# Moving score batches, queue order and the first output parts in a fused linear-attention and local-attention kernel

## The chip, the cores and the metric

The kernel runs on one core of one Trainium2 chip. The metric is the device time of one execution in microseconds (us); every kernel is run several times and the median of its runs is quoted. A profiled execution has a "span", which is about 1.7 us shorter than the time of the same run.

Names used below: PE is the matmul engine, PEld its weight loads, ACT is ScalarE, DVE is VectorE, SP is the engine whose queue issues most DMAs.

## The reference

Two attention blocks over the same input x (2048 x 1024) are mixed by a gate:

```python
g = sigmoid((x * gate_w).sum(-1, keepdims=True))
a = A(x, A_wqkv, A_wo)   # linear attention: phi(q) @ (phi(k)^T v) / den, 32 heads
b = B(x, B_wqkv, B_wo)   # each query sees 8 keys, 2 positions apart (dilated window), softmax
return g * a + (1 - g) * b
```

## The kernel before

It has three stages that matter here. Stage 1 (to 218 us) makes A's keys, values and normalized queries. The *window stage* (218 to 372 us) does B in eight chunks of four heads. Each chunk has two *quads* of 32 steps; a step is four 64x64 matmuls of 512 columns that run side by side and takes 0.216 us. A quad makes the keys `kt` and the queries `qz` of half of the sequence, in four PSUM banks. Between the steps stand, at fixed step numbers, five *score batches* per chunk (query times key, then exp on ACT, mask on DVE) and five *PV batches* (probabilities times V), each 14 steps after its scores. After the first half of an output's sum, one column of its bank is copied to `seen`, and the second half waits for that copy. The *output stage* (372 us to the end) sums, for each of 33 output parts, an A side (8 matmuls, `pqT` times `WoA`) and a B side (8 matmuls, `OBT` times `WoB`).

```python
# window stage: four outputs of a quad share steps; evictions follow the last step of a slot
def step(slot, kt):
    for j in range(2):
        for r in range(2):
            mm((slot + 2 * r) % 4, r, kt, j, slot < 2)       # 4 matmuls, 64x64
    if kt == KT - 1:
        for r in range(2):
            o = (slot + 2 * r) % 4
            if slot < 2:
                nc.vector.tensor_copy(out=seen[:], in_=banks[o][:, 0:1])   # one column
            else:
                outputs[o][2](banks[o])                                   # evict
# ... eviction of a query output: the same bank is read by ACT, then by DVE
nc.scalar.activation(out=qz[:, 0, par, :], in_=ps[:], func=ACT.Copy, scale=qsel[:, 0:1])
nc.vector.tensor_scalar(out=qz[:, 1, par, :], in0=ps[:], scalar1=qsel[:, 1:2], scalar2=None, op0=ALU.mult)
# ... positions of the five batches, in steps from the start of the chunk
p_ = 64 * c + (40, 52, 72, 84, 95)[m // 4]
events.append((p_, lambda g=g: scores(g)))
events.append((p_ + 14, lambda g=g: pv(g)))
# ... after the last batch of a chunk: results to DRAM, then one transposing load
nc.sync.dma_start_transpose(out=OBT[:, c, :], in_=obd[c][0:S, :])
# ... output stage
first = [out_part(*p_) for p_ in parts[:3]]
for k in range(2):                 # A sides of three parts, then their B sides
    for f in first:
        f(k)
```

PE, DVE and ACT run in program order in the window stage; the order of the SP queue is chosen by a scheduler.

Of the kernel before, what the change touches and what calls it, by code (L numbers as in the profile page):

```python
# [11 lines left out]
F32 = mybir.dt.float32  # L12
PE = mybir.EngineType.PE
DVE = mybir.EngineType.DVE
P = 128


# [21 lines left out]
def kernel(  # L39
# [11 lines left out]
    nc = tc.nc  # L51
# [40 lines left out]
    for i in range(4):  # L92
        if i == 2:
            nc.sync.dma_start_transpose(out=xT[:, :, P:2 * P], in_=rows(x, P, 2 * P))
        nc.sync.dma_start(out=WkA[0][:, 2 * i:2 * i + 2, :],
                          in_=A_wqkv[2 * i * P:(2 * i + 2) * P, D:D + 512].rearrange("(kt p) n -> p kt n", p=P))
    for t in range(2, NB):
        nc.sync.dma_start_transpose(out=xT[:, :, t * P:(t + 1) * P], in_=rows(x, t * P, (t + 1) * P))
# [44 lines left out]
    with tc.manual_schedule(engines={PE}):  # L143
# [191 lines left out]
            WqB = load_w("WqB", B_wqkv, 0, "wc")  # L335


        with ExitStack() as s2:
            ps_s = s2.enter_context(tc.tile_pool(name="ps_s", bufs=1, space=bass.MemoryType.PSUM))
            ps_o = s2.enter_context(tc.tile_pool(name="ps_o", bufs=1, space=bass.MemoryType.PSUM))  # L340
# [11 lines left out]
            s2.enter_context(tc.manual_schedule(engines={DVE, mybir.EngineType.Activation}))  # L352


            def quad_units(outputs):



                banks = {}

                def mm(o, r, kt, j, first):
                    if first and kt == 0 and j == 0:
                        banks[o] = ps_pj.tile([P, 512], F32, name="q4_ps", tag="pj")
                    lhsT, rhs, _ = outputs[o]
                    nc.tensor.matmul(banks[o][64 * j:64 * j + 64, :], lhsT=lhsT(r, kt, j), rhs=rhs(r, kt),  # L365
                                     start=first and kt == 0, stop=kt == KT - 1, skip_group_check=not first)
# [5 lines that stand above are left out]
                            mm(o, r, kt, j, slot < 2)  # L372
                    if kt == KT - 1:
                        for r in range(2):
                            o = (slot + 2 * r) % 4
                            if slot < 2:
                                nc.vector.tensor_copy(out=seen[:], in_=banks[o][:, 0:1])  # L377
                            else:
                                outputs[o][2](banks[o])
                for slot in range(4):  # L380
                    for kt in range(KT):
                        yield lambda slot=slot, kt=kt: step(slot, kt)
# [45 lines left out]
            def pv(g):  # L428
                c, m0, n = BATCHES[g]
                pt, base, ns = PT[g % 2], BLOCKS[m0][0], n // 2  # L430
                o2 = ps_o.tile([P, 2, 512], F32, name="o2", tag="o")[:, :, 0:ns * 132] \
                    .rearrange("p a (s i e) -> p a s i e", s=ns, i=4)
                for s_ in range(ns):
                    for i in range(4):
                        for dm in range(2):
                            for par in range(2):
                                m = m0 + 2 * s_ + dm
                                o = BLOCKS[m][0] - base
                                r = slice(64 * par, 64 * par + 64)
                                h = (dm + par) % 2  # L440
                                nc.tensor.matmul(o2[64 * h:64 * h + 64, par, s_, i, :], lhsT=pt[r, i, o:o + 64],  # L441
                                                 rhs=V[r, m, 4 * c + i, :], start=True, stop=True)
                part = m0 >= 8
                if m0 in (0, 8):
                    obs[part] = small.tile([P, 2, 5, P], BF16, name="Ob", tag="Ob")
                Ob = obs[part]
                s0 = m0 // 2 - 4 * part
                rd = small.tile([P, 2, 2, 4, 1], F32, name="rd", tag="rd")
                for a in range(2):
                    nc.vector.reciprocal(out=rd[:, a, 0:ns], in_=o2[:, a, :, :, Dh:Dh + 1])  # L450
                for a in range(2):
                    nc.vector.tensor_tensor(out=Ob[:, a, s0:s0 + ns, :].rearrange("p s (i e) -> p s i e", i=4),
                                            in0=o2[:, a, :, :, 0:Dh],
                                            in1=rd[:, a, 0:ns].broadcast_to([P, ns, 4, Dh]), op=ALU.mult)
                if m0 not in (4, 16):
                    return
                runs = ((0, 1), (1, 4), (2, 3)) if not part else ((8, 1), (9, 4), (10, 4), (17, 1))
                for par in range(2):
                    for m, k in runs:
                        h = (m + par) % 2  # L460
                        q0, w, _ = BLOCKS[m]
                        step = 2 * w if k > 1 else w
                        sl = m // 2 - 4 * part
                        nc.sync.dma_start(
                            out=obd[c][1024 * par + q0:1024 * par + q0 + k * step, :]
                            .rearrange("(s r) d -> r s d", r=step)[0:w],
                            in_=Ob[64 * h:64 * h + w, par, sl:sl + k, :])
                if part:
                    nc.sync.dma_start_transpose(out=OBT[:, c, :], in_=obd[c][0:S, :])

            events = []
            for g, (c, m, n) in enumerate(BATCHES):
                p_ = 64 * c + (40, 52, 72, 84, 95)[m // 4]
                events.append((p_, lambda g=g: scores(g)))
                events.append((p_ + 14, lambda g=g: pv(g)))

            def between(a, b):
                return [(p_ - a, f) for p_, f in events if a <= p_ < b]

            def quad(c, hh):  # L480
                outs = [kq_output(c, par, hh, which, kts[c], qzs[c, hh]) for par in range(2) for which in range(2)]
                return list(quad_units(outs))
            for c in range(KT):
                kts[c] = kpool.tile([P, 2, 1024], BF16, name="kt", tag="kt")
                for hh in range(2):
                    qzs[c, hh] = qpool.tile([P, 2, 2, 512], BF16, name="qz", tag="qz")
                    a = 64 * c + 32 * hh
                    interleave(quad(c, hh), between(a, a + 32))


            WoB = load_w("WoB", B_wo, 0, "wb")
            raw = wpool.tile([P, 4, D], BF16, name="raw", tag="wc")
            fw = wpool.tile([P, 2, D], F32, name="fw", tag="wc")
            lw = wpool.tile([P, 4, D], BF16, name="lw", tag="wa")
# [19 lines left out]

        with ExitStack() as s3:
            work3 = s3.enter_context(tc.tile_pool(name="work3", bufs=3))
            pqT.append(big.tile([P, KT, 1536], BF16, name="pqT1", tag="vV"))
            for r0 in (512, 1024):
                nc.sync.dma_start_transpose(out=pqT[2][:, :, r0 - 512:r0], in_=pqd[r0:r0 + 512, :])  # L519
# [7 lines left out]
                normalize(t, r, pn, fw[:, t % 2, :])  # L527
                nc.sync.dma_start_transpose(out=pqT[2][:, :, (t - 4) * P:(t - 3) * P], in_=pn)

            def out_part(tb, c0, n):  # L530

                st = {}

                def mm(side, c):
                    if side == 0 and c == 0:
                        st["ps"] = ps_pj.tile([P, 512], F32, name="d3_ps", tag="pj")
                    if side == 0:
                        lhsT, W = (pqT[tb // 2][:, c, (tb % 2) * P:(tb % 2 + 1) * P] if tb < 4 else
                                   pqT[2][:, c, (tb - 4) * P:(tb - 3) * P]), WoA
                    else:  # L540
                        lhsT, W = OBT[:, c, tb * P:(tb + 1) * P], WoB
                    nc.tensor.matmul(st["ps"][:, 0:n], lhsT=lhsT, rhs=W[c0 // 512][:, c, c0 % 512:c0 % 512 + n],  # L542
                                     start=(side == 0 and c == 0), stop=(side == 1 and c == KT - 1))
                    if side == 0 or c < KT - 1:
                        return
                    osb = work3.tile([P, 512], BF16, name="osb", tag="e")
                    nc.scalar.activation(out=osb[:, 0:n], in_=st["ps"][:, 0:n], func=ACT.Copy,  # L547
                                         scale=omg[:, tb:tb + 1])
                    nc.sync.dma_start(out=rows(out2, tb * P, (tb + 1) * P)[:, c0:c0 + n], in_=osb[:, 0:n])

                def side(k):
                    for c in range(KT):
# [2 lines left out]

            parts = [(tb, c0, n) for tb in range(NB)
                     for c0, n in ([(0, 512), (512, 512)] if tb < NB - 1 else [(0, 512), (512, 256), (768, 256)])]
            first = [out_part(*p_) for p_ in parts[:3]]
            for k in range(2):
                for f in first:  # L560
                    f(k)
            for i, p_ in enumerate(parts[3:]):
                if i % 2 == 1 and i < 8:
                    qa_late(12 + i // 2)
                f = out_part(*p_)
                f(0)
                f(1)


# [28 lines left out]
```

## Time and profile before

The median was 499.35 us when the prediction was made.

The page, for a span of 498.1 us, gives PE's busy time with its share, and in 40 equal slices PE's busy tenths and the granted clock of PE in tenths.

```profile
PE 473.5 (95%) x5748; PEld 249.3 (50%) x5748; DVE 280.9 (56%) x605; ACT 167.9 (34%) x267; POOL 25.7 (5%) x88
...
PE   7999999999999999999999999999984799999997
...
PEclk9999999999999999999999999999998799999999
```

PE is busy 95% of the span. One slice, the 31st, has less than half (4), and there and in the next the granted clock falls too. The list of PE's waits says what it stood still for (us in total, number of waits, longest one):

```profile
engine line waited for: us in total, times, longest us
PE d_ps L542 <- DMA OBT<-obd: 9.7, 1, 9.7
PE s2b L418 <- DVE qz L400: 5.7, 16, 0.5
PE q_ps L365 <- issue: 1.7, 1, 1.7
...
PE q_ps L365 <- DVE seen L377: 1.2, 2, 0.9
```

The largest is one wait for `OBT` in the output stage. The timeline of the SP queue shows why it was late (start, duration in us, what was issued):

```profile
372.30 4.91 SPq L519 DMA_TRANSPOSE pqT<-pqd  x1
...
379.51 4.58 SPq L519 DMA_TRANSPOSE pqT<-pqd  x1
384.32 2.48 SPq L469 DMA_TRANSPOSE OBT<-obd  x1
```

L519 loads `pqT` for the later A sides, L469 is the last `OBT` transpose; between them stand stores of the window results (L464). The scheduler put both large L519 transposes, 4.91 and 4.58 us of queue time, ahead of it. PE in the same time (timeline of all engines; in brackets the idle time before, and what ended it):

```profile
372.30 5.35 PE L542 MATMUL d_ps<-WoA,pqT 128*128 128x512 bf16 x24
...
388.89 5.98 PE L542 MATMUL d_ps<-WoB,OBT 128*128 128x512 bf16 x17 [9.73 <-DMA OBT<-obd]
```

PE did three A sides (24 matmuls), seven matmuls of the first B side, then stood 9.73 us until the transpose landed. The 17 matmuls after that took 5.98 us instead of 3.7, because the clock was at half (0.50 in the windows view from 385 to 390 us). This is what the Trainium skill says ("TensorE: Matmul & The Clock Gate", Part 1): idleness halves the clock, and some 3.4 us of work restore it; here the slow matmuls, 0.43 us apart, lasted about 4.2 us.

The second item, 16 waits of `s2b` (scores) for `qz`, is seen in every chunk. One of them (timeline of all engines):

```profile
278.39 1.26 ACT L399 ACTIVATE qz<-q_ps,qsel 128x512 bf16<-128x512 f32 x2
...
279.11 1.41 DVE L400 TENSOR_SCALAR qz<-q_ps,qsel 128x512 bf16<-128x512 f32 x2 [0.17 <-ACT qz L399]
...
280.57 0.40 PE L418 MATMUL s2b<-qz,kt 64*64 64x128 bf16 x16 [0.47 <-DVE qz L400]
```

ACT starts the two `qz` evictions at 278.39, DVE's two start 0.72 us later and end at 280.52, and only then can the scores at 280.57 start.

### The profile page before, as it was taken

The page shows a single profiled execution, that of the slowest core. Times are in us where ns is not written, and L with a number is a line of the kernel's source. Part 1 is how long each engine was busy: PE and PEld are TensorE (multiplying, and loading weights), DVE is VectorE, ACT ScalarE, POOL GpSimd, SP SyncE. Part 2 cuts the span into 40 slices and gives each one's busy share as a digit, 9 for nine tenths or more (in the row PEclk, how much of TensorE's full clock was granted, in tenths as well). Part 3 has the DMA queues.
Part 4 walks back from the last instruction along what each step waited for, and adds up shares of the span by engine and source line. Part 5 has one row for each costly group of instructions (what it writes and reads, how often), then busy time and mean ns, then how long its engine had stood idle before and what let it go on. Part 6 is the DMA issues. An engine that isn't in the chain of part 4 may idle for free.

```text
span 498.1 us, 13237 instructions
## 1 busy us (share of the span) xinstructions
PE 473.5 (95%) x5748; PEld 249.3 (50%) x5748; DVE 280.9 (56%) x605; ACT 167.9 (34%) x267; POOL 25.7 (5%) x88
## 2 busy tenths in 40 slices
PE   7999999999999999999999999999984799999997
PEld 4444444445444444446666666666661344444444
DVE  1766699961359999994757666666530089200000
ACT  1333311112533333324455554555430133121221
POOL 3900002201000000000000000000000000000000
PEclk9999999999999999999999999999998799999999
DMA  8999940003452335272144354334589223201101
GB/s 190 176 308 366 348 155 0 1 0 111 142 147 80 128 143 143 95 243 103 33 83 48 66 151 82 42 71 73 97 169 191 67 64 74 64 32 42 43 32 44
DMA packets 98301, 55.41 MB, mean 111 GB/s; under 512 B 69570, under 2 KB 90178, under 8 KB 98242
## 3 DMA queue, kind: packets, MB, share of 16 engines
q1 hardware_dynamic: 98242, 54.56, 42.9%
q8 instruction: 45, 0.74, 0.6%
q14 instruction: 14, 0.11, 0.1%
HBM read 26.10 MB, written 15.86 MB: 84 GB/s over the span
## 4 chain that ended last, share of the span: by engine, by line
PE 69%; DVE 20%; SPq 3%; ACT 3%; issue 3%; DMA 2%; ACTq 0%; DVEq 0%
PE d_ps L542 21%; PE q_ps L365 18%; PE g_ps L201 11%; PE pk_ps L153 11%; DVE qz L400 5%; PE p_ps L276 4%; DVE tmp L141 3%; DVE tmp L293 3%; DVE den L295 3%; DVE tmp L302 3%; ACT qz L399 2%; PE s2b L418 2%; SPq L519 2%; DVE e L140 2%; PE o L441 1%
## 5 line engine op out<-in xcount | busy, mean ns | idle before, releaser
L542 PE MATMUL d_ps<-WoB,OBT 128*128 128x512 bf16 (+1 forms) x264 | 62.6, 382 | 9.7 <-DMA OBT<-obd 9.7
L365 PE MATMUL q_ps<-xT,WkB 64*64 64x512 bf16 x1024 | 70.1, 377 | 0.9 <-DVE seen L377 0.9
L140 DVE TENSOR_SCALAR e<-e 128x512 f32<-128x512 f32 x64 | 28.6, 447 | 65.1 <-ACT e L139 65.1
L365 PE MATMUL q_ps<-xT,WqB 64*64 64x512 bf16 x1024 | 63.2, 376 | 0.3 <-DVE seen L377 0.3
L542 PE MATMUL d_ps<-WoA,pqT 128*128 128x512 bf16 (+1 forms) x264 | 60.3, 373 | 0.0
L276 PE MATMUL p_ps<-WvB,xT 128*128 128x512 bf16 x256 | 57.9, 379 | 0.0
L153 PE MATMUL pk_ps<-WkA,xT 128*128 128x512 bf16 x256 | 55.8, 379 | 2.1 <-DMA WkA<-in_A_wqkv_dram 1.6
L201 PE MATMUL g_ps<-pk,xrow 128*128 128x512 bf16 x256 | 55.4, 379 | 0.0
L547 ACT ACTIVATE osb<-d_ps,omg 128x512 bf16<-128x512 f32 (+1 forms) x33 | 22.2, 674 | 95.8 <-PE d_ps L542 89.6
L423 ACT ACTIVATE PT<-s2b 128x928 bf16<-128x928 f32 (+4 forms) x40 | 34.2, 855 | 56.2 <-PE s2b L418 56.2
L542 PEld LDWEIGHTS <-OBT 128*128 128x128 bf16 x264 | 26.3, 100 | 41.0 <-DMA OBT<-obd 10.2
L312 PE MATMUL p_ps<-WqA,xT 128*128 128x512 bf16 x192 | 43.4, 379 | 0.0
L425 DVE TENSOR_TENSOR PT<-PT,mask 128x928 bf16<-128x928 bf16 (+4 forms) x40 | 23.6, 590 | 34.6 <-ACT PT L423 34.6
L365 PEld LDWEIGHTS <-WqB 64*64 64x64 bf16 x1024 | 33.6, 107 | 16.5 <-issue 0.9
L153 PEld LDWEIGHTS <-xT 128*128 128x128 bf16 x256 | 24.9, 98 | 32.8 <-issue 2.2
L542 PEld LDWEIGHTS <-pqT 128*128 128x128 bf16 x264 | 25.8, 98 | 29.8 <-DMA obd<-Ob 0.4
L201 PEld LDWEIGHTS <-xrow 128*128 128x128 bf16 x256 | 25.0, 98 | 30.2
L276 PEld LDWEIGHTS <-xT 128*128 128x128 bf16 x256 | 24.7, 98 | 30.0 <-issue 0.9
L365 PEld LDWEIGHTS <-WkB 64*64 64x64 bf16 x1024 | 30.7, 107 | 14.0 <-issue 1.8
L139 ACT ACTIVATE e<-pk_ps 128x512 f32<-128x512 f32 x32 | 19.0, 597 | 42.2 <-PE pk_ps L153 42.2
L281 ACT CAST tmp<-p_ps 128x512 bf16<-128x512 f32 x32 | 18.7, 589 | 37.4 <-PE p_ps L276 32.6
L312 PEld LDWEIGHTS <-xT 128*128 128x128 bf16 x192 | 18.8, 98 | 22.6
(58 smaller groups left out, 445.2 us busy)
## 6 DMA issues: line engine op xcount, KB each, us to landing
vd<-tmp SPq DMA_DIRECT2D x16, 264.0 KB
xrow<-in_A_x_dram SPq DMA_DIRECT2D x4, 1024.0 KB
out_dram<-osb SPq DMA_DIRECT2D x31, 128.0 KB
pqd<-tmp SPq DMA_DIRECT2D x12, 256.0 KB
WvA<-in_A_wqkv_dram SPq DMA_DIRECT2D x2, 1024.0 KB
WoA<-in_A_wo_dram SPq DMA_DIRECT2D x2, 1024.0 KB
WvB<-in_B_wqkv_dram SPq DMA_DIRECT2D x2, 1024.0 KB
WqA<-in_A_wqkv_dram SPq DMA_DIRECT2D x2, 1024.0 KB
```

The lines of the kernel that those rows point to most:

```text
L139: nc.scalar.activation(out=e[:], in_=pj[:], func=ACT.Exp)
L140: nc.vector.tensor_scalar(out=e[:], in0=e[:], scalar1=1.0, scalar2=1e-6, op0=ALU.min, op1=ALU.add)
L153: nc.tensor.matmul(pj[:], lhsT=xT[:, kt, t * P:(t + 1) * P], rhs=WkA[half][:, kt, :], start=(kt == 0), stop=(kt == KT - 1))
L201: nc.tensor.matmul(pj[:], lhsT=xrow[:, t, kt * P:(kt + 1) * P], rhs=pk[:, t, half * 512:(half + 1) * 512], start=(t == 0), stop=(t == NB - 1))
L276: nc.tensor.matmul(st["pj"][:], lhsT=xT[:, kt, t * P:(t + 1) * P], rhs=WvB[half][:, kt, :], start=(kt == 0), stop=(kt == KT - 1))
L312: nc.tensor.matmul(st["pj"][:], lhsT=xT[:, kt, t * P:(t + 1) * P], rhs=WqA[half][:, kt, :], start=(kt == 0), stop=(kt == KT - 1))
L365: nc.tensor.matmul(banks[o][64 * j:64 * j + 64, :], lhsT=lhsT(r, kt, j), rhs=rhs(r, kt), start=first and kt == 0, stop=kt == KT - 1, skip_ ...
L400: nc.vector.tensor_scalar(out=qz[:, 1, par, :], in0=ps[:], scalar1=qsel[:, 1:2], scalar2=None, op0=ALU.mult)
L423: nc.scalar.activation(out=pt[:, :, 0:W_], in_=s2b[:].rearrange("p a b s -> p (a b) s")[:, :, 0:W_], func=ACT.Exp, scale=SCALE)
L425: nc.vector.tensor_tensor(out=pt[:, :, 0:W_], in0=pt[:, :, 0:W_], in1=mask[:, None, base:base + W_].broadcast_to([P, 4, W_]), op=ALU.mult)
L542: nc.tensor.matmul(st["ps"][:, 0:n], lhsT=lhsT, rhs=W[c0 // 512][:, c, c0 % 512:c0 % 512 + n], start=(side == 0 and c == 0), stop=(side == ...
L547: nc.scalar.activation(out=osb[:, 0:n], in_=st["ps"][:, 0:n], func=ACT.Copy, scale=omg[:, tb:tb + 1])
```

## The change

The intent: take the score batches away from the `qz` evictions, get `OBT` earlier and give PE more work that does not need it, and keep output stores off the queue that is now in strict order.

```diff
-        nc.sync.dma_start(out=WkA[0][:, 2 * i:2 * i + 2, :],
+        (nc.sync if i else nc.scalar).dma_start(out=WkA[0][:, 2 * i:2 * i + 2, :],   # first weight piece
...
+        queue.enter_context(tc.manual_schedule(engines={SP}))                       # SP in program order
...
-                                nc.vector.tensor_copy(out=seen[:], in_=banks[o][:, 0:1])
+                                (look or nc.vector.tensor_copy)(out=seen[:], in_=banks[o][:, 0:1])
...                                                        # look is ACT's copy in the very first quad
+                    if part and c == KT - 1:               # last chunk: OBT in two halves
+                        nc.sync.dma_start_transpose(out=OBT[:, c, 1024 * par:1024 * par + 1024], ...)
-                if part:
+                if part and c < KT - 1:
                     nc.sync.dma_start_transpose(out=OBT[:, c, :], in_=obd[c][0:S, :])
...
-                p_ = 64 * c + (40, 52, 72, 84, 95)[m // 4]
+                p_ = 64 * c + ((43, 55, 75, 86, 97) if c < KT - 1 else (43, 52, 75, 81, 87))[m // 4]
-                events.append((p_ + 14, lambda g=g: pv(g)))
+                events.append((p_ + (14 if c < KT - 1 else 11), lambda g=g: pv(g)))
...
-            WoB = load_w("WoB", B_wo, 0, "wb")             # both halves after the last chunk
+                if c == KT // 2:                           # first half after chunk 4
+                    WoB = load_w("WoB", B_wo, 0, "wb", only=(0,))
+            WoB += load_w("WoB", B_wo, 0, "wb", only=(1,))
...
+            ps_3 = s3.enter_context(tc.tile_pool(name="ps_3", bufs=4, space=bass.MemoryType.PSUM))
-            first = [out_part(*p_) for p_ in parts[:3]]
+            first = [out_part(i, *p_) for i, p_ in enumerate(parts[:7])]   # odd parts in ps_3
...
-                    nc.sync.dma_start(out=rows(out2, ...)
+                    nc.scalar.dma_start(out=rows(out2, ...)
```

More of the change, by code (lines that the diff above doesn't have):

```diff
@@ L14 @@
 DVE = mybir.EngineType.DVE
+SP = mybir.EngineType.SP
 P = 128
@@ L335 @@
             WqB = load_w("WqB", B_wqkv, 0, "wc")
+        queue = ctx.enter_context(ExitStack())
+        queue.enter_context(tc.manual_schedule(engines={SP}))
         with ExitStack() as s2:
@@ L352, with quad_units @@
             s2.enter_context(tc.manual_schedule(engines={DVE, mybir.EngineType.Activation}))
-            def quad_units(outputs):
+            def quad_units(outputs, look=None):
                 banks = {}
@@ L467, in pv @@
                             in_=Ob[64 * h:64 * h + w, par, sl:sl + k, :])
-                if part:
+                    if part and c == KT - 1:
+                        nc.sync.dma_start_transpose(out=OBT[:, c, 1024 * par:1024 * par + 1024],
+                                                    in_=obd[c][1024 * par:1024 * par + 1024, :])
+                if part and c < KT - 1:
                     nc.sync.dma_start_transpose(out=OBT[:, c, :], in_=obd[c][0:S, :])
@@ L481, in quad @@
                 outs = [kq_output(c, par, hh, which, kts[c], qzs[c, hh]) for par in range(2) for which in range(2)]
-                return list(quad_units(outs))
+                return list(quad_units(outs, look=nc.scalar.copy if c == 0 and hh == 0 else None))
             for c in range(KT):
@@ L528, in qa_late, with out_part @@
                 nc.sync.dma_start_transpose(out=pqT[2][:, :, (t - 4) * P:(t - 3) * P], in_=pn)
-            def out_part(tb, c0, n):
+            def out_part(i, tb, c0, n):
                 st = {}
@@ L535, in mm @@
                     if side == 0 and c == 0:
-                        st["ps"] = ps_pj.tile([P, 512], F32, name="d3_ps", tag="pj")
+                        st["ps"] = ps_3.tile([P, 512], F32, name="e3_ps", tag="p3") if i % 2 else \
+                            ps_pj.tile([P, 512], F32, name="d3_ps", tag="pj")
                     if side == 0:
@@ L548, in mm @@
                                          scale=omg[:, tb:tb + 1])
-                    nc.sync.dma_start(out=rows(out2, tb * P, (tb + 1) * P)[:, c0:c0 + n], in_=osb[:, 0:n])
+                    nc.scalar.dma_start(out=rows(out2, tb * P, (tb + 1) * P)[:, c0:c0 + n], in_=osb[:, 0:n])
                 def side(k):
@@ L561 @@
                     f(k)
-            for i, p_ in enumerate(parts[3:]):
-                if i % 2 == 1 and i < 8:
-                    qa_late(12 + i // 2)
-                f = out_part(*p_)
+            for i, p_ in enumerate(parts):
+                if i < 7:
+                    continue
+                if i % 2 == 1 and i < 15:
+                    qa_late(12 + (i - 7) // 2)
+                f = out_part(i, *p_)
                 f(0)
                 f(1)
+        queue.close()
 _INS = ['A_x', 'A_wqkv', 'A_wo', 'B_x', 'B_wqkv', 'B_wo', 'gate_w']
```

## The prediction

> **What bounds it.** The page gives PE busy 473.5 of 498.1 us (24.6 us idle). The list of PE's waits names 9.7 (one wait of the output stage for the transposed OBT, last head group), 5.7 (16 waits of score matmuls for VectorE's qz), 1.7 (no releaser, "issue", in the last projections), 1.2 (the one-column "seen" copies at the start of the window stage, behind VectorE's normalization), about 3.2 at the start, and about 3 remain after the last matmul. In the timeline the matmuls after the 9.7 us wait come 0.43 us apart instead of 0.216 until 393.1, costing about 2.2 us. That agrees with the Trainium skill, "TensorE: Matmul & The Clock Gate", Part 1: half clock after idleness, back to full after some 3.4 us of work (here about 4.2).
>
> **What the change does.** The matmul count is unchanged.
>
> 1. OBT. Today the scheduler put the two big pqT transposes (4.9 and 4.6 us on the SP queue) ahead of the last OBT transpose; it was issued at 384.3 and landed at 388.9, while PE had only three A sides (5.2 us). With SP in program order it goes ahead of them, in two halves; PE gets seven A sides (7 x 8 x 0.216 = 12.1 us); the last PV comes 11 steps (2.4 us) earlier; one WoB half loads earlier. My SP account, with stores of 0.25-0.57 us, a landing of 2-2.5 and transposes of 1.3-2.4, from the start of the last projections: pqT transposes done at +15.6, first OBT half landed at about +24.5; PE needs it at about +29. Wait gone, slow clock gone: 9.7 + 2.2.
>
> 2. Score batches 2-3 steps later: a step is 0.216 us, so 0.43-0.65 us, against waits of at most 0.5. They are on PE's path (47.85 of 50 us busy, the rest these waits): about 5.5 gained. Kt evictions now stand behind an exp; I estimate their bank is free 0.1-0.3 us before its reuse.
>
> 3. The four first "seen" copies on ScalarE, idle then for 6 us: 1.1 gained.
>
> 4. First weight piece on ScalarE's queue: behind its table load, so not itself earlier, but the second x transpose is issued 0.54 us earlier: 0.5 gained.
>
> 5. Eight banks, stores on ScalarE: it has 0.69 us of eviction and 0.33-0.52 of issue per part, against 1.73 us of PE in the run of seven B sides and 3.45 later. No gain, tail near 3 us.
>
> The 1.7 us "issue" gap falls where WoB and transposes crowd the DMA engines; it may come again: half counted.
>
> Sum: 9.7 + 2.2 + 5.5 + 1.1 + 0.5 + 0.8 = 19.8, all on PE's path. Less 0.3 for small new waits.
>
> **Predicted: 479.9 us (range 477.5 to 484.5).** Faster over 2%: 0.95; within 2%: 0.045; slower: 0.005.
>
> **What would show it.** PE waits for OBT under 1 us and granted clock full across the stage change; no score waits on qz (under 0.5 in total); no wait on "seen"; first continuous matmul run from about 7.5 instead of 8.03.
>
> **What would make it wrong.** SP in strict order can block: the pqT transposes wait for a score batch, and the first A side needs the first of them about 2 us after I expect it landed. OBT could still be late by a few us if transposes run slowly beside the WoB load. Kt evictions behind an exp could make PE wait for banks twice per chunk (16 x 0.2 = 3 us).

## The result, and the profile after

| kernel | median us | lowest to highest | span of the profiled run |
|---|---|---|---|
| before | 500.43 | 499.13 to 502.5 | 498.1 |
| changed | 482.88 | 482.72 to 483.14 | 481.1 |

The ratio is 0.9646, with a 95% interval of 0.9607 to 0.9685. A ratio here is the mean time of one kernel's runs over the mean of the other's of the same rounds, so it is not quite the ratio of the medians quoted. The time lies inside the predicted range, 3 us above the predicted 479.9.

The page after, for a span of 481.1 us:

```profile
PE 472.5 (98%) x5717; PEld 260.4 (54%) x5748; DVE 278.3 (58%) x601; ACT 167.4 (35%) x271; POOL 26.0 (5%) x88
...
PE   8999999999999999999999999999999999999997
...
PEclk9999999999999999999999999999999999999999
```

The hole and the clock dip are gone. PE's waits after:

```profile
PE warm L160 <- DVE onesb L111: 1.1, 1, 1.1
PE pk_ps L154 <- DMA WkA<-in_A_wqkv_dram: 0.7, 1, 0.7
PE q_ps L369 <- DVE qz L404: 0.6, 2, 0.3
PE pk_ps L154 <- DMA xT<-in_A_x_dram: 0.6, 1, 0.6
PE p_ps L277 <- issue: 0.3, 2, 0.2
PE q_ps L369 <- issue: 0.2, 1, 0.2
```

No wait for `OBT`, none of `s2b`, none for `seen`; two waits of projections for `qz` are new, 0.6 us in all. The timeline of the SP queue:

```profile
359.00 8.30 SPq L505 DMA_TRANSPOSE pqT<-pqd  x4
...
373.21 1.19 SPq L473 DMA_TRANSPOSE OBT<-obd  x1
...
379.06 1.19 SPq L473 DMA_TRANSPOSE OBT<-obd  x1
380.31 8.62 SPq L528 DMA_TRANSPOSE pqT<-pqd  x2
```

The two `OBT` halves (L473) are now issued at 373.21 and 379.06, ahead of the large transposes (L528). PE has its seven A sides from 367.36 and goes straight on into the B sides:

```profile
367.36 1.90 PE L552 MATMUL d_ps<-WoA,pqT 128*128 128x512 bf16 x7
...
379.46 1.89 PE L552 MATMUL d_ps<-WoB,OBT 128*128 128x512 bf16 x8
```

Where the 17.0 us of span went, from the starts of the stages in the two timelines:

| stretch | before | after | gained | predicted |
|---|---|---|---|---|
| start to the unbroken run of matmuls | 8.03 | 7.80 | 0.23 | 0.5 |
| window stage, first projection to first A side | 218.68 to 372.30 | 218.45 to 367.36 | 4.71 | 7.4 |
| output stage, to the end of the last matmul | 372.30 to 495.07 | 367.36 to 478.09 | 12.04 | 11.9 |
| after the last matmul | 3.03 | 3.01 | 0.02 | 0 |

(The predicted 7.4 is 5.5 for the scores, 1.1 for `seen`, 0.8 for the gap; 0.3 was taken off the whole.) In the window stage 1.2 us are the waits on `seen`, 1.5 are the gap called issue (1.67 before, 0.21 after). That leaves 2.0 us for the score batches where 5.5 were predicted, though all 5.7 us of their listed waits are gone. The period of a chunk, from the first `kt` eviction of one to that of the next, says the same: 16.98 us before, 16.73 after, 8 x 0.25 = 2.0.

The same quad boundary after (timeline of all engines):

```profile
275.78 1.27 ACT L403 ACTIVATE qz<-q_ps,qsel 128x512 bf16<-128x512 f32 x2 [0.58 <-ACT kt L401]
...
276.50 1.41 DVE L404 TENSOR_SCALAR qz<-q_ps,qsel 128x512 bf16<-128x512 f32 x2 [0.69 <-ACT qz L403]
...
277.61 1.19 PE L369 MATMUL q_ps<-xT,WqB 64*64 64x512 bf16 x12
...
278.43 0.43 PE L422 MATMUL s2b<-qz,kt 64*64 64x128 bf16 x7
```

ACT's `qz` starts at 275.78, DVE's two end at 277.91. The twelve `WqB` matmuls from 277.61 are three steps, the first of the new quad that write into the banks which these evictions read. The scores follow 0.82 us later, although three steps take 0.65. The timeline of the weight loads shows the stop that the matmul records cover up:

```profile
277.97 0.35 PEld L369 LDWEIGHTS <-WqB 64*64 64x64 bf16 x10 [0.46 <-issue]
```

PE stood before its third weight load of that step until 277.97, that is until DVE's second `qz` had ended. So the scores wait no more, and the next projections do, for the same evictions. That was the theory (A) to test; the rival (B) was that the shift won its full 5.5 us and other things of the change cost 3 us in the window stage.

### The profile page after: what moved, and what is told of

It reads as the page before. It is cut to its first block, busy times and chain, and to the rows that moved or that the text cites. A ratio compares the mean times of both kernels' runs of the same rounds, so it can differ in the third digit from the quotient of the medians.

```text
span 481.1 us, 13156 instructions
## 1 busy us (share of the span) xinstructions
PE 472.5 (98%) x5717; PEld 260.4 (54%) x5748; DVE 278.3 (58%) x601; ACT 167.4 (35%) x271; POOL 26.0 (5%) x88
## 4 chain that ended last, share of the span: by engine, by line
PE 93%; DVE 3%; ACT 2%; issue 1%; DMA 1%; SPq 0%
PE q_ps L369 22%; PE d_ps L552 12%; PE p_ps L277 11%; PE g_ps L202 11%; PE pk_ps L154 11%; PE e_ps L552 11%; PE p_ps L313 9%; DVE qz L404 2%; PE s2b L422 2%; PE o L445 2%; DMA xT<-in_A_x_dram 1%; ACT qz L403 1%; ACT kt L401 1%; PE kv_ps L222 0%; PE w_ps L265 0%
## 5 line engine op out<-in xcount | busy, mean ns | idle before, releaser
L369 PE MATMUL q_ps<-xT,WqB 64*64 64x512 bf16 x1024 | 75.8, 378 | 0.9 <-DVE qz L404 0.3
L369 PE MATMUL q_ps<-xT,WkB 64*64 64x512 bf16 x1024 | 70.5, 376 | 0.2 <-issue 0.2
L141 DVE TENSOR_SCALAR e<-e 128x512 f32<-128x512 f32 x64 | 27.6, 431 | 65.3 <-ACT e L140 65.3
L369 PEld LDWEIGHTS <-WqB 64*64 64x64 bf16 x1024 | 38.3, 106 | 18.2 <-issue 7.7
L369 PEld LDWEIGHTS <-WkB 64*64 64x64 bf16 x1024 | 39.8, 107 | 10.1 <-issue 0.9
L552 PE MATMUL d_ps<-WoA,pqT 128*128 128x512 bf16 (+1 forms) x133 | 31.1, 373 | 0.2
L552 PE MATMUL d_ps<-WoB,OBT 128*128 128x512 bf16 (+1 forms) x134 | 31.2, 373 | 0.1
L552 PE MATMUL e_ps<-WoB,OBT 128*128 128x512 bf16 (+1 forms) x125 | 29.1, 372 | 0.2
```

What stands on the lines that cost most here:

```text
L141: nc.vector.tensor_scalar(out=e[:], in0=e[:], scalar1=1.0, scalar2=1e-6, op0=ALU.min, op1=ALU.add)
L369: nc.tensor.matmul(banks[o][64 * j:64 * j + 64, :], lhsT=lhsT(r, kt, j), rhs=rhs(r, kt), start=first and kt == 0, stop=kt == KT - 1, skip_ ...
L552: nc.tensor.matmul(st["ps"][:, 0:n], lhsT=lhsT, rhs=W[c0 // 512][:, c, c0 % 512:c0 % 512 + n], start=(side == 0 and c == 0), stop=(side == ...
```

## The experiments

Each kernel differs from the changed one by the edit shown, unless another is named. Medians of the kernel before in the three sets were 500.93, 501.12 and 501.8 us, and 501.44 in the last. The sets ran on different chips, and the changed kernel was run again in the first set only, so a difference of under a microsecond between sets is not resolved.

### The changed kernel again

> The changed kernel itself, for a base on the same chip. Both theories: 482.9 us within 0.4, ratio to before about 0.965.

482.73 us (482.29 to 483.21), ratio 0.9635. This is the base for the rest.

### Score batches back at their old places

```diff
-((43, 55, 75, 86, 97) if c < KT - 1 else (43, 52, 75, 81, 87))
+((40, 52, 72, 84, 95) if c < KT - 1 else (43, 52, 75, 81, 87))
```

> Only the 2-3 steps later of the score batches of chunks 0 to 6 is taken back. Theory A (the shift won only about 1.8 us, because the qz waits of the scores turned into waits of the next projections for the banks that the qz evictions still read): about 1.6 us slower than the changed kernel, 484.5, with some 5 us of score waits on qz back in the list of PE's waits and no hidden gaps at the first Wq step of a quad. Theory B (the shift won its full 5.5 us, and the missing 3 us were lost elsewhere in the window stage, by interleaving or by kt evictions behind an exp): about 5 us slower, 488.

The median was 487.35 us, which looks like B. But the runs spread from 485.25 to 488.92, and the profiled one (488.54) shows what spreads them:

```profile
314.37 1.73 PE L369 MATMUL q_ps<-xT,WkB 64*64 64x512 bf16 x14 [2.78 <-issue]
```

The windows of 2 us around it (the columns are window, length, busy time of PE, PEld, DVE, ACT and POOL with counts, granted clock, DMA share, GB/s) show half clock after the gap:

```profile
312.00:314.00 2.00, 0.00 (x0) 0.00 (x0) 1.56 (x6) 0.00 (x0) 0.00 (x0) 1.00 0.32 75
314.00:316.00 2.00, 1.63 (x27) 1.19 (x28) 0.00 (x0) 0.00 (x0) 0.00 (x0) 0.65 0.18 41
316.00:318.00 2.00, 2.00 (x32) 1.44 (x30) 0.81 (x3) 0.94 (x1) 0.00 (x0) 0.50 0.00 0
```

The chunk with the gap took 21.15 us, the others 16.98 (16.73 with the shift). Without its excess of 4.2 us this run is 1.7 us slower than the changed kernel without its own 0.2 us gap, and the best run is 2.5 us slower. The score waits on `qz` are back too, 4.5 us in 13. So A holds for the shift in this trace, and the period speaks against B, which needs 5.5 us over eight chunks, 0.69 each, where the shift made 0.25. The rest of this run's difference is the gap, taken up below. The other five runs were not profiled; what they lost is open.

### Crossed evictions

Two query outputs are evicted together, from two banks. As written, DVE's read of a bank waits for ACT's of the same bank, so the chain is ACT, DVE, DVE. The Trainium skill explains the wait ("PSUM — Partial Sum Buffer", section on PSUM bank collisions): no two engines may use one bank in the same partitions at once, reads included, and so software has to keep them apart. The traces agree: DVE's first `qz` began 0.72 us after ACT's in both kernels, at ACT's 0.69 us an eviction. The edit lets each engine start on a bank of its own:

```diff
-                                outputs[o][2](banks[o])
+                                parts_.append(outputs[o][2](banks[o]))     # now returns two closures
+                        if parts_ and parts_[0]:
+                            (a0, a1), (b0, b1) = parts_
+                            for fn in (a0, b1, b0, a1):       # ACT bank 1, DVE bank 2, then swapped
+                                fn()
```

> The changed kernel, with the four qz evictions of a quad crossed: ScalarE starts on one bank while VectorE starts on the other, then they swap; same instructions. Theory A: the two banks are free about 0.4-0.5 us earlier, the gaps at the first Wq step (0.3 and 0.19 us, 16 in all, about 3.9 us) go, and the time falls by 3 to 3.9 us to about 479.4. Theory B: within 0.5 us of the changed kernel.

477.44 us (476.71 to 478.46), ratio 0.9531 (0.9508 to 0.9554): 5.3 us faster than the changed kernel. The same place in its timeline:

```profile
273.21 1.49 DVE L411 TENSOR_SCALAR qz<-q_ps,qsel 128x512 bf16<-128x512 f32 x2
...
273.22 1.46 ACT L409 ACTIVATE qz<-q_ps,qsel 128x512 bf16<-128x512 f32 x2 [0.56 <-ACT kt L406]
...
275.03 0.83 PE L369 MATMUL q_ps<-xT,WqB 64*64 64x512 bf16 x12
...
275.68 0.39 PE L429 MATMUL s2b<-qz,kt 64*64 64x128 bf16 x16
```

Both engines start at 273.2 and are done at 274.70, 1.5 us after, where the chain took 2.1. The projections at 275.03 find their banks free and the scores follow 0.65 us later. The period of a chunk is 15.89 us, 0.84 less; in the two profiled runs the first A side came 5.8 us sooner (361.56 against 367.36), short of 8 x 0.84 in part because an issue gap made one chunk of the crossed run 0.7 us longer. The weight-load waits that the profile can name no releaser for ("issue") tell the story in three kernels. First before, where they are those of the scores (L418):

```profile
PEld L418 <- issue: 9.1, 16, 0.8
```

Then the changed kernel, where the waits are those of the projections (L369):

```profile
PEld L369 <- issue: 9.4, 20, 0.6
```

And the crossed one:

```profile
PEld L369 <- issue: 3.0, 6, 0.8
```

The change moved some 9 us of waiting from one line to another; crossing removed most of it. A is shown. The gain was larger than the 3 to 3.9 us expected: 0.30 + 0.17 us at the two places of a chunk are the direct gaps, and the rest of the 0.84 is spread, for instance over score batches that take 0.58 us from first to last matmul in the changed kernel and 0.39 in the crossed one. Why they are longer after such a wait was not tested.

### Crossed evictions with the old places

Both edits above.

> Crossed evictions and the score batches of chunks 0 to 6 at their old positions. Theory A: the evictions are the root of both waits, so most of the gain comes without any shift; scores at the old places wait at most 0.1 us each: 479.5 to 481. If the shift is needed in its own right: 1.5 us or more slower than the crossed one.

480.02 us (479.21 to 482.2), ratio 0.9588. The period is 16.34 us, and some score waits are back:

```profile
PE s2b L429 <- ACT qz L409: 1.6, 6, 0.3
```

So crossing is worth 0.64 us a chunk at the old places and 0.84 at the new, and the shift 0.25 without crossing and 0.45 with it. The expectation of A ("479.5 to 481") was met, and so was the other one: the shift is also worth 2.6 us in its own right once the evictions are short.

### Crossed evictions on the kernel before

The crossing edit alone, on the kernel before.

> The kernel before, with nothing of the change but the crossed qz evictions. If the eviction chain was already what held PE there: the chunk period falls from 16.98 to about 16.35 us (the difference that crossing made in the changed kernel with old positions), some 5 us in all, 495.5 against 500.9, the wait of 9.7 us for OBT unchanged. If crossing helps only together with the new order: under 1 us.

497.57 us (496.88 to 498.08), ratio 0.9931 (0.9903 to 0.9959): 3.9 us, clear of the noise, though under 2%. The period fell to 16.34 us as expected, so eight chunks gave 5.1. Part of it was given back at the next wait:

```profile
PE d_ps L549 <- DMA OBT<-obd: 12.8, 1, 12.8
```

PE reached the output stage 5.5 us sooner in the profiled runs (366.83 against 372.30), but `OBT` landed only 2.4 us sooner (386.47 against 388.89), so PE waited 12.8 us for it instead of 9.7. The expectation that this wait would not change was wrong.

### SP queue ordered by the scheduler

```diff
-        queue.enter_context(tc.manual_schedule(engines={SP}))
+        pass
```

> The changed kernel, but the scheduler orders the SP queue again (the two big pqT transposes then stand ahead of both halves of the last OBT transpose); seven A sides, late batches and eight banks kept. If the SP order is needed as well as the A sides: the first OBT half is issued at about 381.5 and lands near 384.5, PE needs it near 380.9: a wait of 3 to 4 us for OBT, perhaps some us at half clock after it, 486 to 488 us. If seven A sides alone cover it: no wait, 483.

The queue did what was expected of it, with the large transposes (L528) ahead of the `OBT` halves (L473):

```profile
368.39 4.92 SPq L528 DMA_TRANSPOSE pqT<-pqd  x1
...
375.62 4.14 SPq L528 DMA_TRANSPOSE pqT<-pqd  x1
379.87 2.57 SPq L473 DMA_TRANSPOSE OBT<-obd  x2
```

But the list of PE's waits has none for `OBT` in the profiled run (484.67 us); that run lost 1.5 us in a gap of the issue kind at 360.7. The list of the weight loads' waits has one:

```profile
PEld L552 <- DMA OBT<-obd: 0.6, 1, 0.6
```

PE came to the first use of the last `OBT` piece at about 382.6 (368.97, the start of the A sides, plus 12.1 and 1.5 us). The weight load for it started at 382.82, after 0.58 us of standing, and the second B side began 2.00 us after the first (381.06 and 383.06) instead of 1.73. So PE lost 0.3 us, and the expected wait of 3 to 4 us was wrong. The other runs, 485.68 to 490.65 us, were not profiled, so what they lost is open. Seven A sides alone almost cover the late transpose, with nothing to spare. The program order adds the margin: the first `OBT` half is issued 7.8 us before its first use in the changed kernel (373.21 to about 381.0) and 2.7 us before it here (379.87 to about 382.6).

### Three A sides first

```diff
-            first = [out_part(i, *p_) for i, p_ in enumerate(parts[:7])]
+            first = [out_part(i, *p_) for i, p_ in enumerate(parts[:3])]
```

(with the loop over the later parts moved to match)

> The changed kernel with three A sides first instead of seven; SP in program order kept. In the changed kernel the first OBT half is issued at 373.2 and DMA traffic of it ends near 377; with three A sides PE needs it at 374.05: a wait of 2 to 3 us for OBT[...], about 485.2 us. If the SP order alone did it: no wait, 483.

```profile
PE d_ps L552 <- DMA OBT<-obd: 2.7, 1, 2.7
```

The wait is 2.7 us, as expected, and that run took 486.0 us with the granted clock at 1.0. The other three, at 0.993 to 0.996, took 487.96 to 489.63. So the rest of the change (queue order, halves, early `WoB` half) cut the wait from 9.7 to 2.7, and the four more A sides took what was left. The other three were not profiled; from their mean clock it is argued, not shown, that they had a stretch at half clock after the wait. That a wait of this length should cost half clock in some runs and not in others would fit the Trainium skill, same page and part, which says that the activity window of about 3.4 us is free-running and the slow stretch run-variable.

### Both WoB halves late

```diff
-                if c == KT // 2:
-                    WoB = load_w("WoB", B_wo, 0, "wb", only=(0,))
-            WoB += load_w("WoB", B_wo, 0, "wb", only=(1,))
+            WoB = load_w("WoB", B_wo, 0, "wb")
```

> The changed kernel with both halves of WoB loaded after the last chunk, as before. Theory F (the gaps called issue are PE's instruction block arriving late when DMA is crowded: in four traces they fell after 5087, 3679, 3807 and 3679 weight loads, all 95 modulo 128, so 256 PE instructions apart): no gap near 310, a gap of 0 to 2.8 us near 360, after a load count that is 95 modulo 128 (4959 or 5087), and the time moves by that gap alone, 482.5 to 486, OBT still in time. If the gaps have nothing to do with WoB's load, the one near 310 stays.

A miss of a kind that the prediction had named as a risk: PE waited for `pqT` at its first A side.

```profile
PE d_ps L550 <- DMA pqT<-pqd: 3.8, 1, 3.8
```

The SP queue shows the cause: behind 2 MB of `WoB` the four small transposes took 11.49 us to issue, against 8.30 in the changed kernel, and everything behind them came later:

```profile
360.89 1.04 SPq L81 DMA_DIRECT2D WoB<-in_B_wo_dram  x2
362.05 11.49 SPq L503 DMA_TRANSPOSE pqT<-pqd  x4
...
378.27 1.19 SPq L473 DMA_TRANSPOSE OBT<-obd  x1
```

Two runs at clock 1.0 took 484.41 and 484.88 us, four at 0.993 to 0.996 took 488.1 to 489.9 (median of all 488.16). With the queue in strict order, loading half of `WoB` early is what keeps the first A side in time.

### The gap called issue

In eight traces PE stood still for a while in the window stage with no releaser. The number of weight loads done before the gap, counted in the windows view, was 5087 (before, in the last projections), 3679 (changed, 0.21 us), 3679 (old places, 2.78 us), 3807 (crossed, 0.35 us), 5087 (scheduler's queue, 1.54 us), 5087 (spaced last chunk, 0.4 us), 3679 (first copies on VectorE, 0.98 us) and 5215 (stores on SP, 0.18 us). All of these are 95 modulo 128. (Two gaps of 0.16 us in stage 1, the same in the kernels before and after, do not follow this pattern.) A matmul and its weight load are two instructions, so the gaps lie a multiple of 256 PE instructions apart. The Trainium skill ("Runtime: NRT & Kernel Launch", section on instruction fetch mechanics) says that instructions are fetched by DMA in blocks of 256 and that crossing a block is mostly hidden. The page of each profile agrees on the size: one of its two instruction queues has 45 packets with 0.74 MB, and 45 x 256 is 11,520, for 5748 matmuls with their weight loads (11,496). That the gap is a late instruction block is the reading that fits; no run moved the blocks on purpose, so it is argued and not shown. Each began 5.7 to 8.6 us after a half of `WoB` was issued. The run with both halves late was expected to have no gap near 310 us, and its trace has none; but neither have the changed kernel's second trace and that with three A sides, where the load stood in its usual place, so this decides nothing. One run tried to thin that traffic, with `WoB`'s first half in four pieces after chunks 4 to 7, on the crossed kernel:

```diff
-                if c == KT // 2:
-                    WoB = load_w("WoB", B_wo, 0, "wb", only=(0,))
+                if c == KT // 2:
+                    WoB = [wpool.tile([P, KT, 512], BF16, name="WoB0", tag="wb")]
+                if c >= KT // 2:
+                    k_ = 2 * (c - KT // 2)
+                    nc.sync.dma_start(out=WoB[0][:, k_:k_ + 2, :], in_=B_wo[k_ * P:(k_ + 2) * P, 0:512]...)
```

> The crossed kernel with the first WoB half in four pieces of 256 KB, one after each of chunks 4 to 7, instead of one of 1 MB after chunk 4. Theory F: the 0.35 us gap at 311.5 goes and so does the run-to-run spread of the crossed kernel (476.7 to 478.5): 476.6 within 0.4 us in all runs. Otherwise: 477.4 as before with the same spread.

476.83 us (476.31 to 477.76), ratio 0.9522. The gap at 311.5 is gone in the profiled run, where every chunk from the third on takes 15.88 to 15.89 us, but the spread is 1.45 us against 1.75, so the spread was not explained by that gap alone. The gain over the crossed kernel, 0.6 us, is within their spreads. This version has the lowest median of all, 24 us below the kernel before and 6 below the change.

### Last chunk's batches as far apart as the others

```diff
-(43, 52, 75, 81, 87)        -(14 if c < KT - 1 else 11)
+(43, 55, 75, 86, 97)        +14
```

> The changed kernel with the batches of the last chunk as far apart as those of the other chunks (last PV 13 steps, 2.8 us, later). In the changed kernel the SP queue was busy with the four small pqT transposes until 367.3, some 5 us after the last PV's results were there. So if the queue is what the last stores wait for: no change, 482.8 within 0.5. If the earlier batches are what brought OBT in time: up to 2.8 us later, with a wait for OBT.

482.67 us (481.96 to 484.06), no change, as expected of a queue that is busy. The first `OBT` half was issued at 373.24, against 373.21: in both traces the small `pqT` transposes and the stores behind them hold the queue without a break, to 370.90 here and to 370.99 in the changed kernel. The earlier batches are worth nothing while they do.

### Output stores on the SP queue

```diff
-                    nc.scalar.dma_start(out=rows(out2, ...)
+                    nc.sync.dma_start(out=rows(out2, ...)
```

> The changed kernel with the output stores back on the SP queue, now in program order behind transposes that wait for VectorE. If PE's eight banks absorb the late stores: within 0.6 us of the changed kernel, 482.8. If the stores back up into the evictions: PE waits for banks in the output stage, 1 us or more slower.

483.25 us (482.75 to 483.69), within 0.6 us, and PE waited for no bank in the output stage. Moving the stores to ACT's queue gained nothing that these runs resolve.

### The first one-column copies on VectorE

```diff
-                return list(quad_units(outs, look=nc.scalar.copy if c == 0 and hh == 0 else None))
+                return list(quad_units(outs, look=None))
```

> The changed kernel with the four first one-column copies back on VectorE. PE waits about 0.9 and 0.3 us for them again: 1.1 to 1.2 us slower, 483.9. If the later eviction chain hides it: 482.8.

484.75 us (484.33 to 485.15), 2.0 us slower by the medians, but by the ratios to the kernel before of the same sets (0.966 and 0.9635, with intervals that overlap) 1.3 us. The list of PE's waits has 1.2 us for `seen`, as expected, and 1.0 us of an issue gap, 0.8 more than in the changed kernel. So in the profiled run the copies account for the 1.1 to 1.2 predicted, and the gap for the rest.

## Why the prediction was right or wrong

The time fell inside the range and the direction was sure. That says little for each term: the stated range reached 4.6 us above the predicted time, and the 3.5 us missing from the score term were in part made up by 0.7 us more from the issue gap. Term by term:

- **OBT and the slow clock (9.7 + 2.2).** Right in size: the output stage became 12.0 us shorter. The account named four helpers. The A sides were necessary (2.7 us of wait with three), and the early `WoB` half too (3.8 us of wait for `pqT` without it). The earlier last batches did nothing. Without the program order, seven A sides left 0.3 us of wait in the run profiled. The two halves of the transpose were not tested alone.
- **Score batches (5.5).** This is the step that failed: "They are on PE's path (47.85 of 50 us busy, the rest these waits): about 5.5 gained." The waits were on the path, but the cause, evictions that end 2.1 us after they start, was left as it was, and the next user of the same banks is the step right behind the old place of the scores. The term measured 2.0 us (0.25 a chunk). The prediction did look at bank reuse, but at that of `kt`, which did not wait; it did not check the `qz` banks, for which it had both numbers at hand: 2.1 us of chain plus 0.3 to its start against 8 steps and a PV batch, 1.7 + 0.25 us.
- **`seen` (1.1).** Right: 1.2.
- **First weight piece (0.5).** Mis-sized: 0.23. The second x transpose was issued 0.48 us earlier, at 2.85 against 3.33, but PE's unbroken run started only 0.23 us earlier, at 7.80; the transpose's issue itself took 1.49 us instead of 1.25. The piece itself was issued earlier too, at 0.83, and its first matmuls began at 4.96 instead of 6.18; the prediction had ruled that out.
- **Eight banks and stores on ACT (0).** Right, 3.0 us after the last matmul in both.
- **The issue gap (0.8).** Gained 1.5 in these profiles. It was halved as luck; the runs bear that out, since the same kernel with other positions lost up to 4.2 us to it.

What was to show it came true for `OBT`, for the clock, for `seen` and for the listed `qz` waits (zero of `s2b`). That last sign was a poor one: the list lost its 5.7 us and the stage gained 2.0. The sign of a first unbroken run of matmuls from about 7.5 came half true, at 7.80.

## What to carry to other kernels

When a consumer waits for an eviction, look for the next user of the evicted banks before you move the consumer: moved waits leave the list of waits and stay in the time, and the idle time of weight loads finds them. Shorten the chain itself first; here two engines starting on different banks gave more than moving the consumer (0.84 us a chunk against 0.25). And with a DMA queue in program order, count what stands ahead of each transfer that an engine will wait for, bulk loads included.

## What the Trainium skill lacked or had wrong

- "Trainium Kernel Development and Optimization", Performance Expectations, warns that matmul busy time is a bad metric for how close a kernel is to its roofline. The runs agree: 98% busy in the changed kernel, and 6 us more were to be had. The busy share of the weight loads, one of the two measures that it puts in its place, did not show them either: 54% in the changed kernel and 52% in the faster crossed one. It does not say that weight-load idle time without a releaser finds such waits: 9.4 us in the changed kernel, 3.0 in the crossed one.
- "PSUM — Partial Sum Buffer" says that two engines' reads of one bank must be kept apart, and that ScalarE and VectorE can read PSUM in parallel while no bank collides. It does not draw the consequence that two banks, each read by both engines, can be evicted crosswise: 1.5 us instead of 2.1, worth 5.3 us here.
- "Runtime: NRT & Kernel Launch" calls the crossing of an instruction block mostly hidden. Gaps of 0.18 to 2.78 us at weight-load counts 95 modulo 128 fit a crossing that was not hidden; the cause was argued only.
- No page that was read for this gives the cost of transposing DMAs behind a bulk load on the same queue: four took 8.0 to 9.8 us to issue behind 1 MB (8.30 in the changed kernel) and 11.49 us behind 2 MB.
